# u with interleaved halves, turned by TensorE as float32 words in four whole-array transposes

## The chip, the cores and the metric

One Trainium2 chip, one NeuronCore. The metric is the device time of one execution in microseconds (us), lower is better. Engines are named as in the profile: PE is TensorE (PEld its weight loads), DVE is VectorE, ACT is ScalarE, POOL is GpSimd, SP is SyncE, which issues nearly all DMAs.

## What is computed

Retention attention over 8 batches, 8 heads, 576 tokens and a head size of 64, followed by a SoLU layer with layer norm:

```python
scores = scale * np.matmul(q, k.transpose(0, 1, 3, 2))
ret = scores * Dmat                      # decay gamma ** (i - j) for i >= j, else 0
x = np.matmul(ret, v)                    # (8, 8, 576, 64), then to (4608, 512)
h = x @ w_in                             # (4608, 1024)
e = np.exp(h - h.max(-1, keepdims=True))
solu = h * e / (e.sum(-1, keepdims=True) + 1e-09)
ln = (solu - mean(solu)) / np.sqrt(var(solu) + 1e-06) * g_ln
out = ln @ w_out                         # (4608, 512)
```

Inputs and output are float32. The kernel keeps the operands of its matrix products in float16.

## The kernel before

The 4608 tokens are 36 chunks of 128: four whole ones per batch, and one that holds the last 64 tokens of two batches. Attention runs chunk by chunk with a state that is carried along. For each chunk q, k and v are loaded (`ld`), scaled or cast to f16 (`cq`, `ck`, `cv`), q and k are turned so that the head size lies on partitions (`tq`, or `tr` with a DMA), scores are formed (`sc`), masked (`mk`), multiplied with v (`av`), and the carried state is added (`fs`, from `kv`, `ad`, `dk`, `d3`).

The second part, per chunk: `m1` forms h (128 tokens x 1024) in PSUM, `mx` takes the row maximum, `xp` the exponential, and `so` writes u = -h * e as 128 x 1024 f16 with its row sum. The sum and the squares of u (`sq`) give the norm, which is applied at the end as one scale per row (`ra`, `rp`, `st`). For the first five chunks (`PLAIN`) u is centred in place (`ce`); for later ones w_out is centred instead (`mm`, `mc`, `ws`). For the product with w_out (`m2`, eight blocks of 128 rows of w_out), u must stand with its 1024 features on partitions. There are two ways:

- `du`: a transposing DMA, SBUF to SBUF, for 16 chunks.
- `tu` and `eu`: PE turns u into a bank of PSUM, and ACT or DVE copies it to SBUF as `uT`. 19 chunks go this way. The last chunk goes this way in two halves of 512 (`ht`, `he`, read by `h2`).

PE's instructions here use half the width of the array: `turn` and `product` split each 128 columns of the stationary operand in two of 64 (`HALF`). In the profile such instructions have the form 128*64, and those of `sc`, which use half of the rows, have 64*128.

```python
HALF = (slice(0, 64), slice(64, P))

def turn(out, in_):
    for w in HALF:
        nc.tensor.transpose(out=out[w], in_=in_[:, w], identity=ident)
```

One `tu` is thus 8 x 2 transposes of 64 columns of u, each with a weight load, against the 128x128 f16 identity `ident`. A second identity, `ident32`, is float32, 8x8, and serves one transpose of g_ln (`gt`). Both are made by POOL at the start (`c1`).

The order of all work is written out by hand: `ORDER` is one list of steps with their chunks, from which every engine's queue follows; `BANKS` and `SLOTS` say which PSUM bank and which buffer each step takes. Buffers, banks and order are the same before and after the change.

Of the kernel before, what the change touches and what calls it, by code (L numbers as in the profile page):

```python
# [10 lines left out]
FP = mybir.dt.float32  # L11
F16 = mybir.dt.float16
BF16 = mybir.dt.bfloat16
P = 128
# [9 lines left out]
ORDER = """  # L24
# [73 lines left out]
    e=3, u=5, uT=5, o_sb=4,  # L98
# [48 lines left out]
def kernel(  # L147
# [10 lines left out]
    nc = tc.nc  # L158
# [3 lines left out]
    NF = DFF // P  # L162
    ACT = mybir.ActivationFunctionType
    ALU = mybir.AluOpType
# [4 lines left out]
    const = ctx.enter_context(tc.tile_pool(name="const", bufs=1))  # L169
    load = ctx.enter_context(tc.tile_pool(name="load", bufs=6))  # L170
    half = ctx.enter_context(tc.tile_pool(name="half", bufs=4))
# [3 lines left out]
    utp = ctx.enter_context(tc.tile_pool(name="utp", bufs=3))  # L175
# [35 lines left out]
    warm = const.tile([P, 512], F16, name="warm")  # L211
    ones = const.tile([P, P], F16, name="ones")
    gln = const.tile([NF, P], FP, name="gln")
    ident32 = const.tile([NF, NF], FP, name="ident32")
    g32 = const.tile([P, NF], FP, name="g32")
    w_in32 = const.tile([P, 4, DFF], FP, tag="w32", name="w_in32")
    w_out32 = const.tile([P, NF, DM], FP, name="w_out32")
    w_in16 = const.tile([P, 4, DFF], F16, name="w_in16")
    w_out16 = const.tile([P, NF, DM], F16, name="w_out16")
    gq, gk = small[:, 0:8], small[:, 8:16]  # L220
    gqt, gkt = small[:, 16:24], small[:, 24:32]
    gs = small[:, 32:36]
# [7 lines left out]
    def ring(pool, shape, dtype, name):  # L230

        at = int(next(slots[name]))
        assert at < RINGS[name]
        return pool.tile(shape, dtype, tag=f"{name}_{at}", name=name, bufs=1)

    def bank(shape, dtype, name):
        return ps.tile(shape, dtype, tag="b" + next(banks), name=name)

    ENG = {"a": nc.scalar, "v": nc.vector, "g": nc.gpsimd}
    T = {}  # L240

    def copy(engine, out, in_):
        (engine.copy if engine is nc.scalar else engine.tensor_copy)(out=out, in_=in_)  # L243
# [4 lines left out]
# [5 lines that stand above are left out]
    def product(out, lhsT, rhs, start, stop):  # L253

        for w in HALF:
            nc.tensor.matmul(  # L256
                out=out[w], lhsT=lhsT[:, w], rhs=rhs, start=start, stop=stop,
                skip_group_check=True,
            )
# [263 lines left out]
    def so(n):  # L523

        u = ring(moe, [P, DFF], F16, "u")
        su = tiny.tile([P, 1], FP, name="su")
        nc.vector.scalar_tensor_tensor(  # L527
            out=u, in0=T.pop(("h", n)), scalar=-1.0, in1=T.pop(("e", n)), op0=ALU.mult,
            op1=ALU.mult, accum_out=su,
        )  # L530
        T["u0", n], T["su", n] = u, su
        if n >= PLAIN:
            T["u", n] = T["v", n] = u
# [49 lines left out]

    def tu(n):

        u = T.pop(("u", n))
        lp = bank([P, NF, P], F16, "lp")
        for c in range(NF):
            turn(lp[:, c], u[:, c * P : (c + 1) * P])
        T["lp", n] = lp  # L590

    def du(n):
        uT = ring(utp, [P, NF, P], F16, "uT")
# [1 line left out]
        T["uT", n] = uT  # L595

    def eu(n, e="a"):
        uT = ring(utp, [P, NF, P], F16, "uT")
        copy(ENG[e], uT, T.pop(("lp", n)))
        T["uT", n] = uT  # L600

    def m2(n):

        uT = T.pop(("uT", n))
        o = bank([P, DM], FP, "o")
        assert T["w_out"] == NF and (n < PLAIN or T["w_cen"] == NF)
        w = w_out16 if n < PLAIN else T["w_c"]
        for c in range(NF):
            product(o, uT[:, c], w[:, c], c == 0, c == NF - 1)
        T["o", n] = o  # L610

    def st(n):
# [49 lines left out]
    def ho(n, i):  # L662
        i = int(i)
        u = moe.tile([P, 512], F16, tag="uh", name="uh", bufs=2)
        su = tiny.tile([P, 1], FP, name="suh", bufs=2)
        nc.vector.scalar_tensor_tensor(
            out=u, in0=T.pop(("hh", n, i)), scalar=-1.0, in1=T.pop(("he", n, i)), op0=ALU.mult,
            op1=ALU.mult, accum_out=su,
        )
        T["hsu", n, i] = su  # L670
        T["hu", n, i] = T["hv", n, i] = u
# [5 lines left out]

    def ht(n, i):
        i = int(i)
        lp = bank([P, 4, P], F16, "lph")  # L680
        u = T.pop(("hu", n, i))
        for c in range(4):
            turn(lp[:, c], u[:, c * P : (c + 1) * P])
        T["hlp", n, i] = lp

    def he(n, i, e="v"):
        i = int(i)
        uT = utp.tile([P, 4, P], F16, tag="uTh", name="uTh", bufs=2)
        copy(ENG[e], uT, T.pop(("hlp", n, i)))
        T["huT", n, i] = uT  # L690

    def hq(n, i, e="a"):
# [16 lines left out]
    def h2(n, i):  # L709

        w = slice(256 * int(i), 256 * int(i) + 256)
        o = bank([P, 256], FP, "oh")
        for c in range(NF):
            product(o, T["huT", n, c // 4][:, c % 4], T["w_c"][:, c, w], c == 0, c == NF - 1)
        T["ho", n, i] = o

    def hw(n, i, e):
# [23 lines left out]
    def c1(_):  # L741
        nc.scalar.dma_start(out=small, in_=nc.inline_tensor(small_np, name="small_c").ap())
        nc.scalar.dma_start(out=gln, in_=moe_g_ln.rearrange("(c p) -> c p", p=P))
        nc.gpsimd.memset(ident, 1.0)
        nc.gpsimd.affine_select(
            out=ident, in_=ident, pattern=[[1, P]], channel_multiplier=-1, base=0,
            compare_op=ALU.is_equal, fill=0.0,
        )
        nc.gpsimd.memset(ident32, 1.0)
        nc.gpsimd.affine_select(  # L750
            out=ident32, in_=ident32, pattern=[[1, NF]], channel_multiplier=-1, base=0,
            compare_op=ALU.is_equal, fill=0.0,
        )
        nc.gpsimd.memset(tris[:, 0], 1.0)
        nc.gpsimd.affine_select(
            out=tris[:, 0], in_=tris[:, 0], pattern=[[1, P]], channel_multiplier=-1, base=0,
            compare_op=ALU.is_ge, fill=0.0,
        )
        m = tris[:, 1].rearrange("p (t b) -> p t b", b=2)
        nc.gpsimd.tensor_tensor(  # L760
            out=m, in0=tris[:, 0].rearrange("p (t b) -> p t b", b=2),
            in1=par.unsqueeze(1).to_broadcast([P, 64, 2]), op=ALU.mult,
        )
        nc.vector.memset(warm, 0.0)
        nc.vector.memset(mhalf, -0.5)
        nc.gpsimd.memset(ones, 1.0 / DFF)

    def gt(_):
        T["gT"] = ring(ps_h, [P, DFF], FP, "h")
        nc.tensor.transpose(out=T["gT"][:, 0:NF], in_=gln, identity=ident32)  # L770

    def c2(_):
        nc.vector.tensor_scalar(
# [92 lines left out]
```

## Time and profile before

| | |
|---|---|
| median of 3 runs | 212.85 us (212.41 to 213.39) |
| profiled execution: span, first to last instruction | 210.9 us |
| runs' median over the profiled span | 1.95 us |
| PE busy | 194.3 us, 3125 instructions |
| DVE, ACT, POOL busy | 181.4, 170.5, 157.2 us |
| granted TensorE clock | 1.00 |

For the profiled execution the profile gives its span only; no time with what lies around it was recorded for it, so it is set against the median of the runs. A line of the groups view reads: line of the kernel, engine, operation, output<-inputs with shapes, count, busy time in us, mean length of one in ns, and idle time of the engine before it with what ended it. A matmul's length holds the latency of the pipeline, so starts, not lengths, show how close one follows another. A timeline row is start, length, engine, line, operation, and the count of instructions that it merges. The chain of waits is followed back from the last instruction, each time to what released it.

### The profile page before, as it was taken

How to read it: one execution, taken by the hardware profiler on the slowest of the kernel's cores; microseconds unless marked ns; L12 is line 12 of the kernel's file. 1: busy time of each engine (PE TensorE's matmuls, PEld its weight loads, DVE VectorE, ACT ScalarE, POOL GpSimd, SP SyncE). 2: the span in 40 equal slices, each digit the busy share in tenths (PEclk: the TensorE clock that was granted, in tenths of full speed). 3: DMA queues.
4: the chain of work that ended last, by engine and by line, in shares of the span. 5: the costliest groups of instructions: out<-in, count | busy, mean ns of one | idle time of the engine just before them, and what ended most of it. 6: DMA issues, size and time to landing. Idle time of an engine off the chain costs nothing.

```text
span 210.9 us, 7583 instructions
## 1 busy us (share of the span) xinstructions
PE 194.3 (92%) x3125; PEld 124.0 (59%) x3125; DVE 181.4 (86%) x323; ACT 170.5 (81%) x299; POOL 157.2 (75%) x226
## 2 busy tenths in 40 slices
PE   0887798999999999999999999999999998999992
PEld 0464476575666657657566667575656654565562
DVE  0486999979997999899989999999879998999760
ACT  2424999898979999999898978999679976677981
POOL 5377899676689899888839798879999977545620
PEclk9999999999999999999999999999999999999999
DMA  5999998999898989999999899999989999899754
GB/s 134 257 330 294 258 272 290 253 209 299 224 215 258 265 215 273 221 251 230 208 275 197 205 231 238 273 226 206 179 143 256 210 166 205 156 247 199 154 174 149
DMA packets 110834, 47.71 MB, mean 226 GB/s; under 512 B 94536, under 2 KB 104784, under 8 KB 110800
## 3 DMA queue, kind: packets, MB, share of 16 engines
q1 hardware_dynamic: 110480, 47.07, 99.7%
q8 instruction: 24, 0.39, 0.8%
q10 hardware_dynamic: 320, 0.16, 0.3%
q14 instruction: 10, 0.08, 0.2%
HBM read 32.54 MB, written 9.44 MB: 199 GB/s over the span
## 4 chain that ended last, share of the span: by engine, by line
PE 55%; SPq 14%; DMA 8%; DVE 8%; POOL 7%; ACT 3%; issue 3%; DVEq 0%; POOLq 0%
PE o L256 21%; PE h L256 18%; SPq L274 5%; SPq L270 5%; DMA w_out<-in_moe_w_out_dram 3%; PE tp L251 3%; PE sc L381 3%; PE lp L251 3%; DMA qkT<-k 2%; PE x L456 2%; POOL v L279 2%; SPq L789 2%; DMA qf<-in_q_dram 2%; PE x L256 2%; SPq L779 2%
## 5 line engine op out<-in xcount | busy, mean ns | idle before, releaser
L256 PE MATMUL h<-w_in,xT 128*64 128x512 f16 x560 | 66.9, 380 | 0.1
L256 PE MATMUL o<-w_c,uT 128*64 128x512 f16 x480 | 56.9, 380 | 0.0
L394 DVE TENSOR_TENSOR ret<-sc,tris 128x512 f16<-128x512 f32 x72 | 46.1, 682 | 2.8 <-PE sc L381 2.5
L256 PEld LDWEIGHTS <-xT 128*64 128x64 f16 x576 | 31.5, 110 | 23.1 <-issue 0.7
L512 DVE TENSOR_REDUCE nm<-h 128x1 f32<-128x1024 f32 x35 | 42.6, 1216 | 2.8 <-PE h L256 2.7
L256 PEld LDWEIGHTS <-uT 128*64 128x64 f16 x560 | 31.0, 110 | 23.0 <-issue 0.6
L527 DVE SCALAR_TENSOR_TENSOR u<-h,e 128x1024 f16<-128x1024 f32 x35 | 42.5, 1215 | 1.5 <-ACT e L518 1.4
L518 ACT ACTIVATE e<-h,nm 128x1024 f32<-128x1024 f32 x35 | 39.4, 1125 | 5.0 <-DVE nm L512 3.1
L432 POOL TENSOR_TENSOR s<-t,small 128x512 f16<-128x512 f32 x32 | 33.9, 1063 | 7.4 <-DVE t L420 6.1
L555 ACT ACTIVATE sq<-u,su 128x1024 bf16<-128x1024 f16 x30 | 34.8, 1159 | 2.0 <-DVE u L527 2.0
L581 POOL TENSOR_TENSOR rs<-w,mhalf 128x1 f32<-128x1 f32 x36 | 20.3, 570 | 20.7 <-DVE w L572 17.2
L290 POOL TENSOR_TENSOR q<-qf,small 128x512 f16<-128x512 f32 x30 | 31.2, 1043 | 5.4 <-DMA qf<-in_q_dram 5.1
L279 POOL TENSOR_TENSOR v<-vf,small 128x512 f16<-128x512 f32 x30 | 31.7, 1062 | 2.8 <-DMA vf<-in_v_dram 2.5
L615 ACT ACTIVATE o_sb<-o,rs 128x512 f32<-128x512 f32 x35 | 24.0, 692 | 4.5 <-POOL rs L581 3.2
L243 ACT COPY qkT<-tp 128x512 f16<-128x512 f16 x42 | 23.0, 599 | 5.0 <-PE tp L251 4.9
L243 ACT CAST xT<-x 128x512 f16<-128x512 f32 x29 | 17.1, 593 | 3.1 <-PE x L256 2.8
L251 PE MATMUL tp<-ident,q 128*64 128x128 f16 x232 | 12.4, 230 | 6.0 <-POOL q L290 5.5
L243 ACT CAST k<-kf 128x512 f16<-128x512 f32 x17 | 10.5, 626 | 7.7 <-DMA kf<-in_k_dram 7.7
L456 PE MATMUL x<-ret,v 128*64 128x128 f16 x288 | 14.8, 222 | 2.1 <-DVE ret L394 1.5
L251 PEld LDWEIGHTS <-q 128*64 128x64 f16 x280 | 11.0, 115 | 8.9 <-POOL q L290 5.7
L381 PE MATMUL sc<-qkT 64*128 64x128 f16 x288 | 14.7, 223 | 1.3 <-DMA qkT<-k 0.8
L444 POOL TENSOR_TENSOR s<-t,small 128x256 f32<-128x256 f32 x24 | 15.3, 638 | 0.9 <-DVE t L420 0.8
(87 smaller groups left out, 272.1 us busy)
## 6 DMA issues: line engine op xcount, KB each, us to landing
qf<-in_q_dram SPq DMA_DIRECT2D x36, 256.0 KB, 5.1
kf<-in_k_dram SPq DMA_DIRECT2D x36, 256.0 KB, 5.0
vf<-in_v_dram SPq DMA_DIRECT2D x36, 256.0 KB, 5.5
out_dram<-o_sb SPq DMA_DIRECT2D x35, 256.0 KB, 4.2
w_in<-in_moe_w_in_dram SPq DMA_DIRECT2D x4, 512.0 KB, 6.0
w_out<-in_moe_w_out_dram SPq DMA_DIRECT2D x4, 512.0 KB, 6.5
uT<-u SPq DMA_TRANSPOSE x16, 4.6
out_dram<-o_sbh SPq DMA_DIRECT2D x2, 64.0 KB, 1.8
```

Source lines behind the costliest of these rows:

```text
L243: (engine.copy if engine is nc.scalar else engine.tensor_copy)(out=out, in_=in_)
L251: nc.tensor.transpose(out=out[w], in_=in_[:, w], identity=ident)
L256: nc.tensor.matmul(out=out[w], lhsT=lhsT[:, w], rhs=rhs, start=start, stop=stop, skip_group_check=True,)
L279: engine.tensor_tensor(out=dst, in0=T.pop((key, n)), in1=table.unsqueeze(2).to_broadcast([P, H, D]), op=ALU.mult,)
L290: ENG[e].tensor_tensor(out=dst.rearrange("p (a h) d -> p h a d", h=2), in0=T.pop(("qf", n)).rearrange("p (h a) d -> p h a d", h=2), in1=ta ...
L394: nc.vector.tensor_tensor(out=r, in0=s, in1=m, op=ALU.mult)
L432: nc.gpsimd.tensor_tensor(out=s16, in0=t.unsqueeze(2).to_broadcast([P, 4, 2, D]), in1=gd.unsqueeze(3).to_broadcast([P, 4, 2, D]), op=ALU.mult,
L512: nc.vector.tensor_reduce(out=nm, in_=T["h", n], axis=AX.X, op=ALU.max, negate=True)
L518: nc.scalar.activation(out=e, in_=T["h", n], func=ACT.Exp, bias=T.pop(("nm", n)), accum_out=s)
L527: nc.vector.scalar_tensor_tensor(out=u, in0=T.pop(("h", n)), scalar=-1.0, in1=T.pop(("e", n)), op0=ALU.mult, op1=ALU.mult, accum_out=su,)
L555: nc.scalar.activation(out=s, in_=T.pop(("v", n)), func=ACT.Square, scale=-float(DFF), bias=T.pop(("su", n)), accum_out=ss,)
L615: nc.scalar.activation(out=o_sb, in_=T.pop(("o", n)), func=ACT.Copy, scale=T.pop(("rs", n)))
```

## The change

`so` and `ho` write u with its two halves interleaved: element 2q holds feature q and element 2q+1 feature 512+q (for the half chunk, 256+q), by an output access pattern with a step of two elements. Two neighbouring f16 values are then one float32 word. The new helper `words` turns these words: four float32 transposes of 128 columns per chunk, over the whole array, where there were sixteen f16 ones of 64 columns; in each half of the last chunk two where there were eight. They need a 128x128 float32 identity, so `ident32` grows from 8x8. The bank, read again as f16, holds for each block and partition the pairs of 128 tokens; `eu` and `he` copy it as it stands. Feature block c is then `uT[:, c % 4, :, c // 4]`, every second element, which `m2` and `h2` load as weights by the new helper `paired`. Chunks that go by DMA (`by_dma`) keep u and uT as they were.

```diff
-    ident32 = const.tile([NF, NF], FP, name="ident32")
+    ident32 = const.tile([P, P], FP, name="ident32")
...
+    by_dma = {int(x.split(":")[1]) for x in ORDER.split() if x.startswith("du:")}
...
+        h, e, to = T.pop(("h", n)), T.pop(("e", n)), u
+        if n not in by_dma:
+            h, e = (x.rearrange("p (i q) -> p i q", i=2) for x in (h, e))
+            to = u.rearrange("p (q i) -> p i q", i=2)
         nc.vector.scalar_tensor_tensor(
-            out=u, in0=T.pop(("h", n)), scalar=-1.0, in1=T.pop(("e", n)), op0=ALU.mult,
-            op1=ALU.mult, accum_out=su,
+            out=to, in0=h, scalar=-1.0, in1=e, op0=ALU.mult, op1=ALU.mult, accum_out=su
         )
...
     def tu(n):
 
-        u = T.pop(("u", n))
-        lp = bank([P, NF, P], F16, "lp")
-        for c in range(NF):
-            turn(lp[:, c], u[:, c * P : (c + 1) * P])
-        T["lp", n] = lp
+        T["lp", n] = words(T.pop(("u", n)), 4, "lp")
+
+    def words(u, count, name):
+
+        lp = bank([P, count, P], FP, name)
+        u = u.bitcast(FP)
+        for c in range(count):
+            nc.tensor.transpose(
+                out=lp[:, c], in_=u[:, c * P : (c + 1) * P], identity=ident32
+            )
+        return lp
+
+    def paired(uT, c):
+
+        half = uT.shape[1]
+        return uT[:, c % half, :, c // half]
...
     def eu(n, e="a"):
-        uT = ring(utp, [P, NF, P], F16, "uT")
-        copy(ENG[e], uT, T.pop(("lp", n)))
+        uT = ring(utp, [P, 4, P, 2], F16, "uT")
+        copy(
+            ENG[e], uT.rearrange("p c t i -> p c (t i)"), T.pop(("lp", n)).bitcast(F16)
+        )
...
         for c in range(NF):
-            product(o, uT[:, c], w[:, c], c == 0, c == NF - 1)
+            u = uT[:, c] if n in by_dma else paired(uT, c)
+            product(o, u, w[:, c], c == 0, c == NF - 1)
...
+        h, e = (T.pop((x, n, i)).rearrange("p (i q) -> p i q", i=2) for x in ("hh", "he"))
         nc.vector.scalar_tensor_tensor(
-            out=u, in0=T.pop(("hh", n, i)), scalar=-1.0, in1=T.pop(("he", n, i)), op0=ALU.mult,
+            out=u.rearrange("p (q i) -> p i q", i=2), in0=h, scalar=-1.0, in1=e, op0=ALU.mult,
...
-        for c in range(4):
-            turn(lp[:, c], u[:, c * P : (c + 1) * P])
-        T["hlp", n, i] = lp
+        T["hlp", n, i] = words(T.pop(("hu", n, i)), 2, "lph")
...
-        uT = utp.tile([P, 4, P], F16, tag="uTh", name="uTh", bufs=2)
-        copy(ENG[e], uT, T.pop(("hlp", n, i)))
+        uT = utp.tile([P, 2, P, 2], F16, tag="uTh", name="uTh", bufs=2)
+        copy(
+            ENG[e], uT.rearrange("p c t i -> p c (t i)"),
+            T.pop(("hlp", n, i)).bitcast(F16),
+        )
...
-            product(o, T["huT", n, c // 4][:, c % 4], T["w_c"][:, c, w], c == 0, c == NF - 1)
+            u = paired(T["huT", n, c // 4], c % 4)
+            product(o, u, T["w_c"][:, c, w], c == 0, c == NF - 1)
...
-            out=ident32, in_=ident32, pattern=[[1, NF]], channel_multiplier=-1, base=0,
+            out=ident32, in_=ident32, pattern=[[1, P]], channel_multiplier=-1, base=0,
...
-        nc.tensor.transpose(out=T["gT"][:, 0:NF], in_=gln, identity=ident32)
+        nc.tensor.transpose(out=T["gT"][:, 0:NF], in_=gln, identity=ident32[0:NF, 0:NF])
```

More of the change, by code (lines that the diff above doesn't have):

```diff
@@ L679, in ht @@
         i = int(i)
-        lp = bank([P, 4, P], F16, "lph")
-        u = T.pop(("hu", n, i))
-        for c in range(4):
-            turn(lp[:, c], u[:, c * P : (c + 1) * P])
-        T["hlp", n, i] = lp
+        T["hlp", n, i] = words(T.pop(("hu", n, i)), 2, "lph")
     def he(n, i, e="v"):
         i = int(i)
-        uT = utp.tile([P, 4, P], F16, tag="uTh", name="uTh", bufs=2)
-        copy(ENG[e], uT, T.pop(("hlp", n, i)))
+        uT = utp.tile([P, 2, P, 2], F16, tag="uTh", name="uTh", bufs=2)
[3 more added lines that the diff above has]
+        )
         T["huT", n, i] = uT
```

## The prediction

> **What bounds the kernel now.** I read the page first, then busy time by stage, then the chain of waits, and last TensorE's own timeline around the step that changes.
>
> ```profile
> span 210.9 us, 7583 instructions
> PE 194.3 (92%) x3125; PEld 124.0 (59%) x3125; DVE 181.4 (86%) x323; ACT 170.5 (81%) x299; POOL 157.2 (75%) x226
> PE 55%; SPq 14%; DMA 8%; DVE 8%; POOL 7%; ACT 3%; issue 3%; DVEq 0%; POOLq 0%
> ...
> 49.00:88.00 39.00, 39.00 (x672) 24.81 (x668) 36.24 (x66) 36.66 (x63) 34.13 (x44) 1.00 1.00 246
> 88.00:104.00 16.00, 15.81 (x280) 10.23 (x272) 15.60 (x25) 14.79 (x28) 12.64 (x20) 1.00 1.06 232
> ...
> 179.00:207.00 28.00, 28.00 (x366) 16.51 (x360) 22.55 (x47) 22.40 (x43) 12.86 (x22) 1.00 0.89 187
> ```
>
> The first three lines are the span, busy time by engine, and the chain's shares. In the last three, behind a stage's length, stand the busy times of PE, PEld, DVE, ACT and POOL, then the granted clock. TensorE (PE) is busy for all 39.00 us of 49 to 88 and all 28.00 us of 179 to 207, at clock 1.00, and it carries 55% of the chain. What is added to PE there is added to the end. In 88 to 104 DVE has 15.60 of 16.00 us, and a little more PE work can hide behind it.
>
> The step that changes is the turn of u on PE, in 19 chunks (`tu`) and once in two halves (`ht`): 20 bursts. In the chain in order of time (start, length), the wait that ends its early part and the first and last of these bursts are
>
> ```profile
> 31.84 7.28 DMA w_out<-in_moe_w_out_dram
> 51.32 0.45 PE lp L251 x16
> 203.16 0.45 PE lph L251 x16
> ```
>
> and between these two bursts stand 11 more, so 13 of 20 bursts lie on the chain. The other seven are four between 27 and 40 us, where the chain is SyncE's issuing and then the arrival of w_out from 31.84 on, and three in stages that DVE or POOL carries.
>
> **The turn before.** PE's timeline: start, length with pipeline latency, instruction. The start of the next row shows what a burst really occupies.
>
> ```profile
> 30.48 0.61 PE L251 MATMUL lp<-ident,u 128*64 128x128 f16 x16
> 31.03 0.40 PE L381 MATMUL sc<-qkT 64*128 64x128 f16 x8
> 31.36 0.62 PE L256 MATMUL w<-warm 128*64 128x512 f16 x4
> ...
> 55.95 0.61 PE L251 MATMUL lp<-ident,u 128*64 128x128 f16 x16
> 56.40 0.29 PE L405 MATMUL kp<-v,k 128*64 128x64 f16 x8
> 56.52 0.39 PE L251 MATMUL tp<-ident,q 128*64 128x128 f16 x8
> 56.75 0.39 PE L251 MATMUL tp<-ident,k 128*64 128x128 f16 x8
> ...
> 104.57 0.64 PE L256 MATMUL x<-qkT,s 128*64 128x64 f16 x16
> 104.99 0.44 PE L251 MATMUL tp<-ident,q 128*64 128x128 f16 x8
> ```
>
> From 55.95 to 56.40: a burst of 16 takes 0.45 us. The two halves of the array run at the same time, so that is 8 pairs of 128 columns at 56 ns. That is what the change removes, 0.45 us per burst.
>
> **The switch of array form.** From 56.52 to 56.75, 8 instructions of 128 columns take 0.23 us when the form stays 128*64. The 8 of `sc`, also 4 pairs of 128 columns, are in the form 64*128 and take 0.33 us (31.03 to 31.36); the burst ahead of them has 0.55 us (30.48 to 31.03) instead of 0.45. So each change of form costs about 0.10 us, once on the way in and once on the way out. The new transposes use the whole array, a form between neighbours that are all 128*64 or 64*128. Reading the neighbours of the 20 bursts off the timeline: 9 stand between two 128*64 groups and gain two switches, 11 stand beside an `sc`, where one switch is paid already, and gain one; 29 in all, 18 of them at the 13 bursts of the chain (5 with two, 8 with one). At 0.105 us, the mean of what the two rows give, that is +1.9 us on the chain. No row shows a switch between 128*64 and the whole array. Its bounds are 0 (a switch that leaves the rows whole needs no pause) and 0.15 us (the 0.10 and a longer first load); I take 0.105, since the one whole-width instruction of the trace, below, has pauses of such a size on both sides.
>
> The Trainium skill, TensorEngine Tiling, Key Properties, says that changing the tiling mode, and not just the tile, drains TensorE; by that rule the switch to the whole array is charged as well, and the sum is the one with 1.9 us in it, while without it the sum is near zero. The rows of `sc` agree with it for the forms that occur.
>
> **The four transposes of words.** The only float32 transpose of the trace is the one of g_ln:
>
> ```profile
> L770 PE MATMUL h<-ident,gln 8*128 8x8 f32 x1 | 0.2, 223 | 0.0
> L770 PEld LDWEIGHTS h<-ident,gln 8*128 8x128 f32 x1 | 0.1, 133 | 0.0
> L251 PEld LDWEIGHTS <-u 128*64 128x64 f16 x304 | 10.1, 110 | 2.5
> 15.17 0.32 PE L405 MATMUL kp<-v,k 128*64 128x64 f16 x8
> 15.42 0.22 PE L770 MATMUL h<-ident,gln 8*128 8x8 f32 x1
> 15.57 0.40 PE L381 MATMUL sc<-qkT 64*128 64x128 f16 x8
> ```
>
> It is one instruction with one load. Behind the 8 of `kp`, which occupy 0.12 us (56.40 to 56.52), it starts 0.13 us late, and `sc` starts 0.15 us after it. It doesn't show the rate for 128 columns of 4 bytes. Lower bound: 56 ns each, as a pair of 16-bit turns, 4 x 56 = 0.22 us. Upper bound: nothing overlaps, 4 x 223 ns = 0.89 us. Between them stands the stream with a stride: `x<-qkT,s` of 64 columns in steps of two elements, 4 bytes apart, does 8 pairs in 0.42 us (104.57 to 104.99), 52 ns for 64 columns, where the 64 contiguous columns of `kp` go by at 4 pairs in 0.12 us, 30 ns. So 4 bytes per step run at about half the columns per ns; 128 columns then take 105 ns and a burst 0.42 us. This is the row nearest to a moving operand of float32 words, and I take it. The first load after a switch is exposed; 128 float32 columns took 133 ns against 110 for 64 of 16 bits, +0.02 us per burst. The other three loads lie under the transpose before.
>
> Sum per burst without switches: -0.45 + 0.42 + 0.02 = -0.01 us, so 16 instructions become 4 and PE is no freer. On the chain: 13 x (-0.01) + 1.9 = **+1.8 us**. Off the chain, 7 bursts and 11 switches add 1.1 us that DMA, SyncE, DVE and POOL cover; without that cover it is 1.1 us more.
>
> **What else moves.** The same 1024 f16 values per partition are copied out of the same bank, contiguous on both sides, so `eu` and `he` keep their time. `m2` and `h2` now load weights in steps of two elements:
>
> ```profile
> L256 PEld LDWEIGHTS <-uT 128*64 128x64 f16 x560 | 31.0, 110 | 23.0 <-issue 0.6
> 203.44 1.89 PE L256 MATMUL o<-w_c,uT 128*64 128x512 f16 x16
> 205.17 1.91 PE L256 MATMUL oh<-w_c,uTh 128*64 128x256 f16 x32
> ```
>
> The 16 loads of a burst go by in its 0.45 us, 28 ns each. If the step costs what it cost the stream (52 for 30), a load becomes about 52 ns and the two of a pair 0.105 us. A pair of `m2` lasts 1.73 us / 8 = 0.216 us (203.44 to 205.17), which hides them. A pair of `oh` has half the columns, 0.108 us, which just does. So zero; with the cover gone 16 x 24 ns = 0.38 us per chunk.
>
> VectorE writes u with a step of 4 bytes. No row has such a write; the nearest are copies that read in steps:
>
> ```profile
> L243 DVE COPY qkT<-tp x16: 412/679/691, 7.5 to 190.7; 128x512 f16<-128x512 f16 x16
> L527 DVE SCALAR_TENSOR_TENSOR u<-h,e 128x1024 f16<-128x1024 f32 x35 | 42.5, 1215 | 1.5 <-ACT e L518 1.4
> L666 DVE SCALAR_TENSOR_TENSOR uh<-hh,eh 128x512 f16<-128x512 f32 x2 | 1.4, 692 | 0.9 <-ACT eh L657 0.9
> ```
>
> Contiguous, 512 elements take 412 ns, in steps 679: the steps push a 16-bit copy down to about one element per cycle. The product that writes u is there already, (1215 - 692) / 512 = 1.02 ns per further element, so I put the step at zero. At worst it costs what the copy lost, 2 x 267 = 534 ns per u. A gain is excluded, since the same elements are read.
>
> GpSimd makes a 128x128 float32 identity in place of an 8x8:
>
> ```profile
> 1.31 0.09 POOL L749 MEMSET ident<- 8x8 f32 x1
> 1.47 0.18 POOL L750 TENSOR_SCALAR_AFFINE_SELECT ident<-ident 8x8 f32<-8x8 f32 x1
> 1.60 0.19 POOL L754 MEMSET tris<- 128x128 f32 x1
> 1.87 0.29 POOL L755 TENSOR_SCALAR_AFFINE_SELECT tris<-tris 128x128 f32<-128x128 f32 x1
> 4.41 1.04 POOL L290 TENSOR_TENSOR q<-qf,small 128x512 f16<-128x512 f32 x1 [1.21 <-DMA qf<-in_q_dram]
> ```
>
> That is (0.19 + 0.29) - (0.09 + 0.18) = +0.21 us, ahead of 1.21 us in which POOL waits for q: zero, and 0.21 if q came early. No DMA is added or moved, and no step changes its place in the order.
>
> The profiled span is 210.9 us; the median of the runs, 212.85, stands 1.95 above it, for what lies around the span, which the change leaves alone. 212.85 + 1.8 = 214.65, so **214.7 us**. About 0.5%, 1.06 us, is what a measurement of this kernel can tell from no change.
>
> **The rivals.** *The words pass at full pace, the switch is free* (the other side). Each transpose takes 56 ns and the array goes from halves to whole without a pause: 13 x (-0.45 + 0.22 + 0.02) = -2.7 us, 210.1 us. For it: the step's half pace was seen with two streams at once, and one float32 stream may have what those two shared. Against it: the pauses on both sides of the g_ln transpose. With the switches paid, the point from which it decides is 13 x (4t - 0.43) + 1.9 = 0, t = 71 ns per transpose; below that the change gains.
>
> *Full pace, switches paid.* -2.7 + 1.9 = -0.8 us, 212.0 us: no difference to be told. What speaks for it is the pace of the 16-bit turns on one side and `sc` on the other.
>
> In the Trainium skill, TensorE: Matmul & The Clock Gate, Terms, transpose mode is given as four times as fast for FP32; if that brings words to the pace of 16-bit columns, this rival is what happens. The single instruction with its single load for g_ln agrees, its rate for 128 columns is in no run here.
>
> *The words pass slowly.* Weights of 4 bytes keep load and transpose from overlapping: 0.89 us per burst, 13 x (0.89 - 0.45 + 0.02) + 1.9 = +7.9 us, 220.7 us. For it, 223 ns for a mere 8 columns; against it, every such length in the trace holds some 170 ns of latency that streams overlap (a 128-column turn, too, is shown with 0.39 us for 8 that go by in 0.23).
>
> *A strided operand comes out into the open.* Weight loads not hidden in `m2`: PE o has 21% of the chain (L256), about 44 us or 25 groups, of which 20 in 36 are chunks turned by PE, so 14 x 0.38 = +5.3 on top, 220.0 us. Or the write of u: 0.53 us for each of some 8 u on DVE in 49 to 88, where it has 2.76 us idle, leaves 1.5 us, and in 88 to 104 about 1.5 more: 217.7 us. Slack of 0.11 us per pair speaks against the first, the pace of 1.02 ns per element against the second.
>
> ```profile
> PE o L256 21%; PE h L256 18%; SPq L274 5%; SPq L270 5%; DMA w_out<-in_moe_w_out_dram 3%; PE tp L251 3%; PE sc L381 3%; PE lp L251 3%; DMA qkT<-k 2%; PE x L456 2%; POOL v L279 2%; SPq L789 2%; DMA qf<-in_q_dram 2%; PE x L256 2%; SPq L779 2%
> ```
>
> **How the numbers follow.** Forecast 0.42; full pace with switches 0.22; full pace and free switch 0.15; slow words 0.12; strided operands 0.09. Faster: 0.15 and 0.06 of the second, where the switch costs less than I read, 0.21. Same: its other 0.16 and 0.09 of the forecast, where the busy engines beside PE take up part of the 1.8 us, 0.25. Slower: the rest of the forecast, 0.33, with 0.12 and 0.09, 0.54. The range leaves out the slow words and about half of the free switch: 210.5 to 218.5. The forecast and its neighbour alone, with the switch anywhere between 0 and 0.15 us (18 x 0.15 = 2.7), span 210.1 to 215.5.
>
> **What would show it.** PE has 4 records of lp per chunk in place of 16. Right: from the first lp to the next group between two 128*64 neighbours about 0.65 us, of which the four starts lie 0.105 apart, and the group behind starts late. Wrong to the good: starts 0.056 apart and no pause, 0.25 us. Wrong to the bad: starts over 0.2 apart. If `m2` groups last over 1.73 us or u's writes over 1.25 us, the step costs on the reader's or the writer's side. If PE's bursts are as forecast and the time stands still, DVE and ACT, not PE, set the stages from 49 to 135 us.

## The result, and the profile after

The changed kernel is slower: 214.96 us (214.73 to 215.18, 4 runs) against 212.63 us (211.27 to 213.39, 4 runs), ratio 1.013 with an interval of 1.008 to 1.0179. Measured twice more it had 1.0149 (1.0098 to 1.0201) and 1.0139 (1.0093 to 1.0185). The forecast was 214.7 us. Medians in this document are over all runs of a kernel and ratios over those in the chip's fast state alone, so a ratio need not be the quotient of the two medians beside it. The page after, with two stages of it:

```profile
span 213.1 us, 7108 instructions
PE 196.2 (92%) x2885; PEld 120.4 (56%) x2885; DVE 185.1 (87%) x323; ACT 171.4 (80%) x299; POOL 157.8 (74%) x226
PE 53%; POOL 12%; SPq 11%; DVE 9%; DMA 7%; issue 5%; ACT 1%; DVEq 0%; POOLq 0%
...
0.00:27.00 27.00, 16.21 (x245) 10.40 (x247) 15.77 (x31) 12.52 (x21) 17.62 (x30) 1.00 1.00 253
49.00:88.00 39.00, 38.85 (x572) 23.41 (x569) 36.54 (x66) 35.66 (x60) 32.68 (x41) 1.00 0.98 246
```

PE has 240 instructions fewer and is busy 1.9 us longer. Up to 27 us, ahead of any burst, it is busy 1.5 us less than before (16.21 for 17.71), so from there on it is busy 3.4 us longer. Its timeline shows why; start, length, instruction, once between two 128*64 groups and once behind an `sc`:

```profile
55.29 1.89 PE L257 MATMUL o<-w_out,uT 128*64 128x512 f16 x16
57.12 0.66 PE L597 MATMUL lp<-ident,u 128*128 128x128 f32 x4
57.71 0.32 PE L406 MATMUL kp<-v,k 128*64 128x64 f16 x8
...
62.53 0.40 PE L382 MATMUL sc<-qkT 64*128 64x128 f16 x8
62.85 0.66 PE L597 MATMUL lp<-ident,u 128*128 128x128 f32 x4
63.44 1.92 PE L257 MATMUL h<-w_in,xT 128*64 128x512 f16 x16
```

Rows of the kernel before to set beside these: its first stage, a product and a burst between two 128*64 groups, and a burst behind an `sc`:

```profile
0.00:27.00 27.00, 17.71 (x251) 11.28 (x253) 16.09 (x31) 12.64 (x21) 17.71 (x30) 1.00 1.01 254
...
54.22 1.89 PE L256 MATMUL o<-w_out,uT 128*64 128x512 f16 x16
55.95 0.61 PE L251 MATMUL lp<-ident,u 128*64 128x128 f16 x16
...
83.00 0.64 PE L251 MATMUL lp<-ident,u 128*64 128x128 f16 x16
83.47 1.89 PE L256 MATMUL h<-w_in,xT 128*64 128x512 f16 x16
```

From 55.29 to 57.12 the product ahead occupies 1.83 us instead of 1.73 (54.22 to 55.95): the switch to the whole array, 0.10 us. From 57.12 to 57.71 the burst of four occupies 0.59 us, where the sixteen had 0.45. Between two 128*64 groups a burst is thus longer by 0.24 us. Behind `sc`, whose 0.32 us hold a switch that was there before, the step from burst to next group is 0.59 against 0.47 (83.00 to 83.47 before), 0.12 us more; ahead of an `sc` it is 0.14. The sums below take 0.13 for both. The group behind a burst mostly lasts another 0.02 us longer, which they leave out.

The same burst cut into its first two, three and four transposes, with the view by tile:

```profile
57.12 0.44 PE L597 MATMUL lp<-ident,u 128*128 128x128 f32 x2
57.12 0.55 PE L597 MATMUL lp<-ident,u 128*128 128x128 f32 x3
L597 PE MATMUL lp<-ident,u x76: 272/273/332, 27.6 to 171.4; 128*128 128x128 f32 x76
L597 PEld LDWEIGHTS lp<-ident,u x76: 137/140/143, 27.6 to 171.3; 128*128 128x128 f32 x76
```

With 0.273 us for the second, it starts 0.44 - 0.273 = 0.17 us after the first, and each further one adds 0.11 us to the length (0.44, 0.55, 0.66). So four words occupy 0.17 + 3 x 0.11 = 0.49 us, and the remaining 0.10 of 0.59 is the switch out. The 273 ns of one stand 54 above the 219 of a 16-bit turn of 128 columns.

On DVE the write of u shows two lengths, in steps and contiguous (a chunk that goes by DMA):

```profile
107.58 1.31 DVE L532 SCALAR_TENSOR_TENSOR u<-h,e 128x1024 f16<-128x1024 f32 x1
113.22 1.22 DVE L532 SCALAR_TENSOR_TENSOR u<-h,e 128x1024 f16<-128x1024 f32 x1
```

And POOL's start, with the larger identity:

```profile
1.30 0.20 POOL L768 MEMSET ident<- 128x128 f32 x1
1.58 0.29 POOL L769 TENSOR_SCALAR_AFFINE_SELECT ident<-ident 128x128 f32<-128x128 f32 x1
4.52 1.04 POOL L291 TENSOR_TENSOR q<-qf,small 128x512 f16<-128x512 f32 x1 [1.42 <-DMA qf<-in_q_dram]
```

The first bursts of the two profiles start nearly together (27.41 and 27.63). From the burst at 51.15 (52.18 after) to the one at 130.99 (133.82) the lag grows from 1.03 to 2.83 us, by 1.80. Eleven bursts lie between, five with two new switches and six with one: 5 x 0.24 + 6 x 0.13 = 1.98 us. PE's own bursts thus account for what is lost there, in a stretch where the chain of the profile after is led over POOL and DVE for a good part, while PE is busy for 38.85 of the 39 us from 49 to 88. Behind it the lag falls again, to 1.96 us at the last burst (202.99 and 204.95), for which this pair of profiles gives no reason.

### The profile page after: what moved, and what is told of

It is laid out like the page before. It is cut to its first block, busy times and chain, and to the rows that moved or that the text cites. A ratio compares the mean times of both kernels' runs of the same rounds, so it can differ in the third digit from the quotient of the medians.

```text
span 213.1 us, 7108 instructions
## 1 busy us (share of the span) xinstructions
PE 196.2 (92%) x2885; PEld 120.4 (56%) x2885; DVE 185.1 (87%) x323; ACT 171.4 (80%) x299; POOL 157.8 (74%) x226
## 4 chain that ended last, share of the span: by engine, by line
PE 53%; POOL 12%; SPq 11%; DVE 9%; DMA 7%; issue 5%; ACT 1%; DVEq 0%; POOLq 0%
PE o L257 20%; PE h L257 17%; DMA qf<-in_q_dram 7%; SPq L275 5%; SPq L271 5%; POOL v L280 4%; PE sc L382 3%; PE tp L252 3%; PE lp L597 2%; POOL q L291 2%; PE x L457 2%; PE x L257 2%; POOL s L445 2%; DVE ret L395 2%; POOL rs L585 2%
## 5 line engine op out<-in xcount | busy, mean ns | idle before, releaser
L532 DVE SCALAR_TENSOR_TENSOR u<-h,e 128x1024 f16<-128x1024 f32 x35 | 44.5, 1271 | 1.6 <-ACT e L519 1.5
L257 PEld LDWEIGHTS <-xT 128*64 128x64 f16 x576 | 30.8, 110 | 25.1 <-issue 2.2
L257 PEld LDWEIGHTS <-uT 128*64 128x64 f16 x560 | 30.4, 110 | 24.5 <-issue 1.6
L433 POOL TENSOR_TENSOR s<-t,small 128x512 f16<-128x512 f32 x32 | 34.4, 1077 | 9.5 <-DVE t L421 7.8
L280 POOL TENSOR_TENSOR v<-vf,small 128x512 f16<-128x512 f32 x30 | 31.1, 1043 | 3.0 <-DMA vf<-in_v_dram 2.6
L252 PEld LDWEIGHTS <-q 128*64 128x64 f16 x280 | 10.5, 113 | 9.2 <-POOL q L291 5.9
```

Of the source, the lines that this page charges most:

```text
L257: nc.tensor.matmul(out=out[w], lhsT=lhsT[:, w], rhs=rhs, start=start, stop=stop, skip_group_check=True,)
L280: engine.tensor_tensor(out=dst, in0=T.pop((key, n)), in1=table.unsqueeze(2).to_broadcast([P, H, D]), op=ALU.mult,)
L433: nc.gpsimd.tensor_tensor(out=s16, in0=t.unsqueeze(2).to_broadcast([P, 4, 2, D]), in1=gd.unsqueeze(3).to_broadcast([P, 4, 2, D]), op=ALU.mult,
L532: nc.vector.scalar_tensor_tensor(out=to, in0=h, scalar=-1.0, in1=e, op0=ALU.mult, op1=ALU.mult, accum_out=su)
```

## The experiments

Two theories. *Bursts*: the loss is PE's, the form of the array and not the words. *Write*: DVE's 0.10 us more per u decides, and PE's bursts are taken up elsewhere. The runs come in three sets, which the expectations name calls; each has runs of the kernel before of its own, on another chip.

**First set: the parts one by one.** In this set the runs of the kernel before ranged from 211.4 to 216.23 us (median 213.88), so that its ratios tell less than their intervals say.

Words without the strided write:

```diff
-        if n not in by_dma:
-            h, e = (x.rearrange("p (i q) -> p i q", i=2) for x in (h, e))
-            to = u.rearrange("p (q i) -> p i q", i=2)
...                                          # and the same in ho, for the last chunk
```

> The words without the strided write: u is written contiguously, the rest as in the changed kernel (features end up in another order, so the output is another; the work is the same). Burst theory: the whole loss is PE's bursts, 0.135 to 0.235 us longer each by the trace (0.10 switch in, 0.49 for four words, 0.10 switch out, against 0.45), 13 of 20 on the chain: +1.9 us, ratio 1.009 to 1.013, as slow as the changed kernel within 0.4 us, though u's write is back at 1.21 us. Write theory: DVE's 0.10 us more per u (1.32 against 1.21, 19 chunks) carries at least half of the loss: at most +1.1 us, ratio 1.005 or less.

Measured: 214.59 us, ratio 1.0004 (0.9968 to 1.004). That spoke for the write theory and against mine; but the trace had the same bursts of 0.59 us, and the medians differed by 0.71 us. It was repeated below.

The strided write alone, in the kernel before:

```diff
-            out=u, in0=T.pop(("h", n)), scalar=-1.0, in1=T.pop(("e", n)), op0=ALU.mult,
+            out=to, in0=h, scalar=-1.0, in1=e, ...   # to, h, e as in the change
...                                          # and the same in ho, for the last chunk
```

> The strided write alone: the kernel before, but u of the 19 chunks and of the last one is written with its halves interleaved (turned and read as before, so the features meet the wrong rows of w_out; the work is the same). u's write takes 1.32 us in 19 chunks. Burst theory: within 0.5 us of before, ratio 0.998 to 1.002, since DVE is off the chain where PE is busy throughout. Write theory: +1 us or more, ratio 1.005 to 1.009, with more DVE in the chain.

Measured: 213.42 us, ratio 0.9965 (0.9924 to 1.0006). No loss beside the runs of this set: the write theory's +1 us is not seen.

The strided weights alone, in the kernel before:

```diff
-            product(o, uT[:, c], w[:, c], c == 0, c == NF - 1)
+            product(o, uT[:, c] if n in by_dma else paired(uT, c), w[:, c], ...)
...                                          # the same in h2; eu and he copy into tiles of that shape
```

> The strided weights alone: the kernel before, but m2 and h2 load uT of the 20 bursts in steps of two elements (which blocks meet which rows of w_out is wrong by that; the work is the same). Both theories: m2 stays at 1.73 us and the time within 0.3 us of before, ratio 0.998 to 1.002. If loads came out into the open: m2 up to 0.38 us longer, ratio up to 1.025.

Measured: 212.98 us, ratio 0.9973 (0.9928 to 1.0018). PE's timeline of this kernel, from a product with strided weights to the burst behind it:

```profile
55.67 1.89 PE L257 MATMUL o<-w_out,uT 128*64 128x512 f16 x16
57.40 0.61 PE L252 MATMUL lp<-ident,u 128*64 128x128 f16 x16
```

1.73 us, as with contiguous weights: the loads stay hidden. `oh`, where the prediction saw them just hidden, keeps its 1.91 us in the changed kernel (from 207.29 on).

The form alone, f16 turns over the whole array:

```diff
         for c in range(NF):
-            turn(lp[:, c], u[:, c * P : (c + 1) * P])
+            nc.tensor.transpose(out=lp[:, c], in_=u[:, c * P : (c + 1) * P], identity=ident)
...                                          # and the same in ht, for the last chunk
```

> The form alone: the kernel before, but the turns of u are eight whole-array f16 transposes of 128 columns per chunk (four per half of the last chunk); layout and result are those of before. Burst theory with the switch as its price: 8 x 0.056 = 0.45 us as before plus a switch of 0.10 us on each side that had none, 18 on the chain: +1.9 us, ratio 1.006 to 1.011. Rival, that the float32 word itself is the price: no switch is paid for an f16 turn between halves, and the time is that of before, ratio 0.998 to 1.002.

Measured: 214.03 us, ratio 1.0027 (0.9988 to 1.0066), between the two expectations; repeated below.

**Second set: more of it, and the switch removed.**

> The changed kernel once more, beside the other runs of this call. Burst theory: PE's bursts are longer by 0.14 to 0.24 us and most of that reaches the end, +1.8 to +2.5 us, ratio 1.008 to 1.013. Rival, the parts as measured alone (words 1.0004, strided write 0.9965, strided weights 0.9973, whole form 1.0027): they sum to no loss, and the first measurement of 1.013 owed something to the few runs of the kernel before; ratio 0.997 to 1.004.

Measured: 215.0 us, ratio 1.0149 (1.0098 to 1.0201). The loss stands; the parts of the first set don't sum to it.

Every word transposed twice:

```diff
-        for c in range(count):
+        for c in [*range(count), *range(count)]:
```

> The changed kernel with every word transposed twice into the same place: 4 x 0.107 = 0.43 us more PE per burst, no further switch, the result as before. If what PE's bursts gain reaches the end: 13 x 0.43 = +5.6 us over the changed kernel, ratio to before 1.03 to 1.04. If the engines beside PE take up half and more of it: +2.8 us or less, ratio to before 1.01 to 1.025.

Measured: 221.12 us, ratio 1.0437 (1.0388 to 1.0487), 6.1 us over the changed kernel of the same set. A burst of this kernel:

```profile
58.20 1.10 PE L597 MATMUL lp<-ident,u 128*128 128x128 f32 x8
59.23 0.32 PE L406 MATMUL kp<-v,k 128*64 128x64 f16 x8
```

1.03 us in place of 0.59, so 0.44 for four further words: 0.11 us each, without a second switch. Twenty bursts make 8.8 us, of which 6.1 reach the end, 0.70. That is the exchange rate of PE time in bursts for time at the end, a little over the 13 of 20 that the chain gave.

All turns and products over the whole array, in the changed kernel and in the one before:

```diff
-    HALF = (slice(0, 64), slice(64, P))
+    HALF = (slice(0, P),)
```

> The changed kernel with all turns and products over the whole array (128 columns at a time, half as many instructions), so that the words stand between neighbours of their own form and only the scores still switch. Burst theory: the 18 switches of the chain, 1.9 us, are gone, a burst takes 0.06 + 4 x 0.107 = 0.49 us against 0.45, so +0.5 us, ratio 1.000 to 1.004, if m1 and m2 keep 1.73 us. Rival, that loads of 128 columns come out into the open: m1 and m2 over 1.73 us, by up to 8 x 0.05 = 0.4 us each, ratio over 1.02.

> Control: the kernel before with all turns and products over the whole array. If the halves were worth nothing, ratio 0.997 to 1.003 with m1 and m2 at 1.73 us; with the rival of the run before, over 1.02.

Measured: 219.83 us, ratio 1.0361 (1.0313 to 1.0409), and 219.57 us, ratio 1.0363 (1.0317 to 1.0408). Both are slower by far, so the expectation of +0.5 us fell, but not by the rival that was named: `m1` and `m2` keep their 1.73 us. PE's timeline of the first, then of the second:

```profile
55.25 1.89 PE L257 MATMUL o<-w_out,uT 128*128 128x512 f16 x8
56.98 0.60 PE L597 MATMUL lp<-ident,u 128*128 128x128 f32 x4
57.51 0.32 PE L406 MATMUL kp<-v,k 128*64 128x64 f16 x8
...
60.03 0.41 PE L457 MATMUL x<-ret,v 128*64 128x128 f16 x8
60.38 0.62 PE L257 MATMUL x<-qkT,s 128*128 128x64 f16 x8
```

```profile
55.39 1.89 PE L256 MATMUL o<-w_out,uT 128*128 128x512 f16 x8
57.12 0.61 PE L251 MATMUL lp<-ident,u 128*128 128x128 f16 x8
57.66 0.32 PE L405 MATMUL kp<-v,k 128*64 128x64 f16 x8
```

`kv` and `av` write one head per half and remain 128*64. I had overlooked them: each is now an island with a switch on both sides. From 60.03 to 60.38 the 8 of `av` occupy 0.35 us, where 8 of 128 columns took 0.23 without a switch. Between the fifth and the sixteenth burst of the kernel before and of its whole-array version, `kv` and `av` together grow from 5.6 to 8.4 us, start to start, 2.8 of the 4.2 us lost there; the rest was not taken apart. What the pair does show is the change without its extra switches. The product ahead of the burst keeps 1.73 us (no switch in), four words and one switch out take 0.53 us, eight f16 turns and one switch out 0.54, and the two kernels have the same time within 0.3 us, with the strided write and the strided weights in one of them. With no switch ahead, the first word holds nothing back: 4 x 0.11 + 0.10 is 0.54, with nothing over.

**Third set: the contested parts beside each other.**

> The changed kernel, as the measure for the other runs of this call: ratio 1.008 to 1.015 by its two measurements so far (1.013, 1.0149).

> Words without the strided write, now in one call with the changed kernel (it had 1.0004 in a call where runs of the kernel before ranged from 211.4 to 216.2 us). Burst theory: within 0.5 us of the changed kernel, ratio 1.008 or more. Write theory (the bursts alone are taken up elsewhere, and DVE's 0.10 us per u on top makes the loss): at least 1.2 us below the changed kernel, ratio 1.005 or less.

> Whole-array f16 turns in the kernel before, in one call with the changed kernel: bursts 0.55 us and 0.10 us of entry, by its first trace, against 0.59 and 0.10 for the words. Burst theory: 0.04 us per burst, 0.5 us, below the changed kernel, ratio 1.006 to 1.011. If the switches are taken up by other engines: 1.003 or less.

Strided write for all 36 chunks, in the changed kernel:

```diff
-        if n not in by_dma:
+        if True:
```

> The changed kernel with the strided write for all 36 chunks, those that go by DMA too (their features then stand in another order, so the output is another): 16 more u take 1.32 us on DVE instead of 1.21, most of them between 95 and 200 us. Burst theory: within 0.5 us of the changed kernel. Write theory: as much again as the write of the 19 chunks costs, at least +1 us.

Measured, against 211.82 us: the changed kernel 214.82 us, ratio 1.0139 (1.0093 to 1.0185); words without the strided write 214.61 us, 1.014 (1.0094 to 1.0186); whole-array f16 turns 214.04 us, 1.0105 (1.0054 to 1.0156); the write everywhere 215.28 us, 1.0156 (1.0112 to 1.02). The write of u in the second and in the fourth, by tile (shortest, median, longest in ns):

```profile
L529 DVE SCALAR_TENSOR_TENSOR u<-h,e x35: 1206/1214/1225, 23.2 to 198.4; 128x1024 f16<-128x1024 f32 x35
```

```profile
L532 DVE SCALAR_TENSOR_TENSOR u<-h,e x35: 1290/1317/1344, 23.2 to 198.5; 128x1024 f16<-128x1024 f32 x35
```

Taking the strided write away, with u back at 1214 ns, gives nothing (0.2 us between medians), and putting it on 16 more u costs 0.46 us, inside the interval. The bursts of the f16 turns over the whole array, with the product ahead:

```profile
56.50 1.89 PE L256 MATMUL o<-w_out,uT 128*64 128x512 f16 x16
58.32 0.62 PE L589 MATMUL lp<-ident,u 128*128 128x128 f16 x8
58.87 0.32 PE L405 MATMUL kp<-v,k 128*64 128x64 f16 x8
```

1.82 and 0.55 us against 1.73 and 0.45: one switch on either side, without a single word, in a kernel whose only other difference is half as many instructions in the turn. It has 1.05 of the 1.39% lost. The rest, 0.8 us between medians, is of the size of the 0.04 us by which a burst of words is longer (0.59 against 0.55; 20 of them make 0.8 us, 0.6 at the rate of 0.70), but the two intervals overlap.

**One stretch in every profile.** PE's timelines settle what the medians leave open. The table has the starts of the fifth and of the sixteenth burst, and the time between them, in us; for kernels with several profiles, in the order of their sets:

| kernel | fifth burst | sixteenth | between |
|---|---|---|---|
| before | 51.15 | 130.99 | 79.84 |
| strided write alone | 51.94 | 131.85 | 79.91 |
| strided weights alone | 52.60 | 132.69 | 80.09 |
| whole-array f16 turns | 52.99; 53.42 | 134.30; 134.73 | 81.31; 81.31 |
| words without the strided write | 53.97; 51.88 | 135.63; 133.54 | 81.66; 81.66 |
| changed kernel | 52.18; 53.98; 52.19 | 133.82; 135.63; 133.84 | 81.64; 81.65; 81.65 |
| strided write everywhere | 51.65 | 133.37 | 81.72 |
| every word twice | 52.83 | 138.86 | 86.03 |

Where a kernel has several profiles, the stretch repeats to about 0.01 us. The changed kernel loses 1.8 us in it, and just as much without the strided write; f16 turns over the whole array lose 1.47 of it, and the words add 0.34, near the 11 x 0.04 us of the bursts. The strided write alone costs 0.07 us and the strided weights alone 0.25, by one profile each. So the burst theory stands, and the write theory falls. Of the 11 x 0.44 = 4.8 us of the second turn of the words, 4.4 are lost here, 0.9 and not 0.70: the share depends on the stretch.

What scatters is the way up to the fifth burst, 51.15 to 53.98 us, in kernels of every kind. The profile of the words in the first set has the full loss in the stretch, so their ratio of 1.0004 doesn't mean that the bursts were taken up. Words and f16 turns had the same medians in the first set as in the third (214.59 and 214.61; 214.03 and 214.04); what differed was the kernel before, 213.88 against 211.82. Why it did stays open.

No tried version is faster than the kernel before clear of the noise. Words over halves of the array, which would need no switch, were not run.

## Why the prediction was right

- **The total.** 214.7 against 214.96 us looks closer than it is: the kernel before came out at 212.63 instead of 212.85, and the change cost 2.3, 2.5 and 3.0 us in its three measurements, not 1.8. The mechanism was right and the sum too small, by the two terms named below.
- **The removed bursts, 0.45 us, 13 of 20 on the chain.** Right in kind. Twice the words brought 0.70 of the added PE time to the end, against 13 / 20 = 0.65.
- **The switch, 0.105 us, also between halves and whole array.** Right: 0.10 us on either side, in the bursts of words and in those of f16. The mean of the two rows that the prediction used is 0.10 as well, not 0.105, which makes 1.8 us of its 1.9. This was the step with no row behind it, and the rival without it, 210.1 us, fell with it. The Trainium skill's TensorEngine Tiling (Array Packing), Key Properties, states that a change of the tiling mode drains TensorE. The trace agrees for this pair of forms by its pause of 0.10 us; that the array drains in it is not shown.
- **The rate, 105 ns per transpose.** Right: 0.11 us, in part by luck. The row that it was taken from, `x<-qkT,s`, has its output in steps too and adds to what its bank holds, while the words are contiguous; that the two have one cause is not shown. Nor is it shown whether the stream of 128 columns or the load of 128 float32 columns (140 ns long) sets the 0.11. The rival at 56 ns, 212.0 us, and the slow words at 220.7 us fell. The Trainium skill's TensorE: Matmul & The Clock Gate, Terms, gives transpose mode as "4× faster for FP32". Here this does not bring words to the pace of 16-bit columns: 0.11 against 0.056 us.
- **The first word, 0.02 us exposed.** Too small: 0.17 - 0.11 = 0.06 us, behind a switch. By the measured lengths the 13 bursts of the chain lose 5 x 0.24 + 8 x 0.13 = 2.2 us, not 1.8.
- **The cover for the other seven, 1.1 us.** Only in part. All 20 bursts lengthen by 9 x 0.24 + 11 x 0.13 = 3.6 us; at 0.70 that is 2.5 us. The medians differ by 2.3, 2.5 and 3.0 us. These two terms are what the sum of 1.8 lacks, as far as single medians with intervals of about 1 us on either side can tell.
- **The strided weights at zero.** Right: 1.73 us per product, and `oh` as before.
- **The strided write at zero.** Wrong by itself: 1.31 against 1.22 us, within the bound given (0.53) and over the 1.25 us that the prediction had set as the sign of it. That the product has nothing to lose from steps does not hold; it lost 8%. The time shows nothing of it: the stretch between the bursts has 81.66 us without it and 81.65 with it.
- **The identity, 0.21 us on POOL.** Right: POOL still waits 1.42 us for q behind it.

## What to carry to other kernels

Count PE's work by what it occupies from start to start, and count the changes of array form: here 0.10 us each, as much as two 16-bit turns of 128 columns. Four wide instructions in place of sixteen gained nothing here, since they took as long as those and brought a form of their own between their neighbours. Where one engine is busy for whole stages, check the share of its added time that reaches the end by a run that adds a known amount to it: here 0.70, where the chain of one profile gave 0.65. And where runs scatter, set the same stretch of every profile side by side: here it repeats to 0.01 us, while the medians move by a microsecond.

## What was not expected of the hardware

VectorE's product of two float32 inputs, at 1.02 ns per further element, still takes 1.31 in place of 1.22 us when its 16-bit output is written in steps of 4 bytes. A first float32 transpose behind a switch takes 0.17 us until the next one starts, 0.06 more than the 0.11 us of the others; without a switch ahead it doesn't (0.53 us for four and a switch out).
